# ScalarE's exp planned at its completion rate, accumulator copies on either engine, the tail's range checks in pieces, and the planner's ranks tuned again, in a four-layer attention kernel with a built-in planner

## Chip, cores and metric

One core of a Trainium2 chip. The metric is the device time of one execution in microseconds (us); the kernel before takes **1503.88 us** (median of 3 runs, 1503.73 to 1510.52). A difference under 2% counts as "same", so nearly everything below is about differences that count as the same; some are several times their own noise, some hardly above it, and the text says which.

## The reference, cut

Four residual layers on x (1 x 2048 x 512, bfloat16): two kinds, A and B, in the order A, B, A, B.

```python
x = x + _A_ref(_layernorm(x), A_wqkv, A_wo)   # windowed: 8 keys at distance 2, 32 heads of 16
x = x + _B_ref(_layernorm(x), B_wq, B_wk, B_wv, B_wo)
... # the same two again

def _B_ref(x, wq, wk, wv, wo):                # full attention, 32 heads of 16, one k and v for all
    q = (x @ wq).reshape(B, S, H, Dh).transpose(0, 2, 1, 3)
    k = x @ wk
    v = x @ wv
    scores = jnp.einsum("bhqd,bkd->bhqk", q, k) * (Dh ** -0.5)
    p = _softmax(scores, axis=-1)
    o = jnp.einsum("bhqk,bkd->bhqd", p, v)
    return o.transpose(0, 2, 1, 3).reshape(B, S, H * Dh) @ wo
```

The cost is B: 2 layers x 32 heads x 2048 x 2048 scores and as many exponentials.

## The kernel before

The scores are made in tiles of 128 keys by 512 queries, 4096 of them. A tile is exponentiated in one of two ways: by ScalarE's exp, two tiles an instruction, or by a bit trick: VectorE copies the scores to 16-bit integers, and VectorE or GpSimd adds offsets to them (`do_pass`), so that three shifted sums read as half-precision floats approximate the exponential.

Which tile goes which way, and in which order every engine's instructions are issued, is settled while the program is built. A **planner** in the kernel walks along with a clock for each engine, books each operation at a fixed cost, and always takes the candidate with the lowest start plus bias. The biases ("ranks" from here on) are some fifty tuned numbers. The hardware then runs each engine's list in that order, with semaphores between them; nothing is decided again at run time.

```python
SPAN, ACTIVE = 3413.0, 0.74            # idle matmuls are put in where TensorE is less active than this in such a span
SLACK, PATIENCE = 798.0, 70.6
...
class Stream:
    BIAS = {"act": -50.0, "act2": 1946.7, "vec": 438.1, "pv": 246.6, "pv_in": 177.5, "batch": 17, "few": 19.9,
            "copy": 1.6, "pass": 76.2, "lag": -1045.1, "both": 216.8, "next": 634.6, "late": 31.8, "open": 54.2,
            "close": 4.0}
    ...
    def exp(self, s, _):
        _, key, slot, tiles = self.exps.pop(0)
        n = len(tiles)
        t = 426.7 * n + 52             # the booked cost: 905 ns for two tiles
        S.run("act", s, t)
        done = s + t + LAT["act"]
        S.give(("slot", "exp"), slot, done)
    ...
        # io.exp: nc.scalar.activation(out=pt[:, 0:n, :], in_=st[:, 0:n, :], func=Exp, scale=E_SCALE)
```

A finished accumulator (a PSUM bank of 128 x 512) goes to SBUF; its first part is copied, the others are added:

```python
        def evac(op):
            o = self.o.pop(bank)
            self.chain("dve", nc.vector.tensor_copy(out=X.t[:], in_=o[:]) if fresh else
                       nc.vector.tensor_tensor(out=X.t[:], in0=X.t[:], in1=o[:], op=ALU.add))

        e = X.used(self.op("dve", 599.0, evac, X.prev if fresh else list(X.cur), after=when, frees=[held], prio=-224.4))
```

The approximations hold only in a range of the scores, so the kernel gathers sums and reciprocals (`see`, on GpSimd) and at the very end makes one flag of them, on which an exact fallback branches. Everything behind the last score tile is in `close_tail`:

```python
class Checks:
    def flag_most(self, ok):                       # five flags, one reduction
        ...
        out = [v.tensor_scalar(out=ok[:, at:at + n], in0=x, scalar1=lim, scalar2=None, op0=ALU.is_lt)
               for at, n, x, lim in ((0, 256, self.a[:], self.LOG_A ** 2), (256, 32, self.b[:, 0, :], self.SUM_B),
                                     (288, 32, self.b[:, 1, :], self.REC_B), (320, 512, self.t[:, 0, :], self.SUM_B),
                                     (832, 512, self.t[:, 1, :], self.REC_B))]
        return [*out, v.tensor_reduce(out=self.mb[:, 0:1], in_=ok[:, 0:1344], axis=AX.X, op=ALU.min)]
    ...                                            # flag_last: the last reciprocals' flag and its reduction
    def close_tail(self, a, evac):
        ...                                        # sums by a matmul, Ln, Exp (reciprocal), mult: ons
        self.op("dve", 2300.0, most, [evac, *self.seen, *sees], prio=LATER)
        ...                                        # four output matmuls and their adds
        rec.used(self.op("dve", 1500.0, last, adds))    # flag_last, count (matmul), chk_bad
```

## Time and profile before

| of the kernel before | value | read from |
|---|---|---|
| span of the profiled run | 1500.2 us | head of the page |
| mean granted clock of TensorE | 0.994 | view of the cores |
| exps of two tiles | 1359 | groups |
| tiles by the bit trick | 1378 | groups |
| ScalarE (ACT) idle in all | 1500.2 - 1437.1 = 63.1 us | busy time |

The page's busy times, the groups, the waits and the end of the chain are in the prediction below with their lines.

### The profile page before, as it was taken

Reading aid. Unit: us, or ns where it says so; the run is one execution under the profiler, and the core shown is the slowest. Engines: PE = TensorE matmul, PEld = TensorE weight load, DVE = VectorE, ACT = ScalarE, POOL = GpSimd, SP = SyncE. Lnnn points to the kernel's source line nnn. Section 1 sums busy time; section 2 is a strip of 40 time slices with the busy share of each in tenths; the row PEclk is TensorE's granted clock in tenths of the full one; section 3 lists DMA queues with packets and bytes.
Section 4 is the critical chain, followed back from the end, with each engine's and each line's share of the span. In section 5 each row is a group of like instructions: output and inputs, shape, how many; then the busy total and the mean of one; then the engine's idle time right before and its main releaser. Section 6 shows DMA issues by size and latency. Waiting matters only on the chain.

```text
span 1500.2 us, 42220 instructions
## 1 busy us (share of the span) xinstructions
PE 1430.8 (95%) x17204; PEld 494.9 (33%) x17263; DVE 1339.5 (89%) x2301; ACT 1437.1 (96%) x1754; POOL 896.9 (60%) x741
## 2 busy tenths in 40 slices
PE   8899999999999999999999999999999999999996
PEld 4534343223422233222333224322222222222222
DVE  5787868998799978999789997899999999999997
ACT  6899999999999999999999999999999999999995
POOL 3745546565566656666575664757566656665664
PEclk9999999999999999999999999999999999999999
DMA  4010110011010020100201001001000000000000
GB/s 142 5 29 3 30 16 16 17 31 34 14 23 13 17 38 7 27 13 16 35 13 27 13 15 16 16 9 43 27 12 14 13 23 17 9 18 20 16 9 24
DMA packets 84114, 32.95 MB, mean 22 GB/s; under 512 B 71688, under 2 KB 77448, under 8 KB 83912
## 3 DMA queue, kind: packets, MB, share of 16 engines
q1 hardware_dynamic: 83048, 28.33, 8.8%
q8 instruction: 137, 2.24, 0.6%
q10 hardware_dynamic: 864, 1.84, 0.3%
q14 instruction: 65, 0.53, 0.1%
HBM read 13.53 MB, written 2.61 MB: 11 GB/s over the span
## 4 chain that ended last, share of the span: by engine, by line
ACT 45%; PE 42%; issue 7%; DVE 4%; POOL 1%; DMA 0%; ACTq 0%; POOLq 0%; DVEq 0%
ACT pt L1481 40%; PE o L1507 14%; PE st L1466 14%; PE y L1130 3%; ACT P L1353 2%; PE q L1130 2%; PE k L1130 2%; PE qb L1130 2%; DVE t L1485 2%; PE v L1297 1%; PE dv L1466 1%; ACT logs L1403 1%; ACT rec L1405 1%; PE st L1346 1%; DVE i L1495 1%
## 5 line engine op out<-in xcount | busy, mean ns | idle before, releaser
L1481 ACT ACTIVATE pt<-st 128x1024 bf16<-128x1024 f32 x1359 | 1271.8, 1168 | 16.9 <-PE o L1507 9.1
L1490 POOL TENSOR_TENSOR i<-t,off 128x1024 int32<-128x1024 int32 x345 | 656.2, 1904 | 488.1 <-DVE i L1495 332.7
L1485 DVE TENSOR_SCALAR t<-dv 128x512 int16<-128x512 f32 x1378 | 877.9, 683 | 51.3 <-PE dv L1466 41.5
L1466 PE MATMUL st<-QT,KAB 32*128 32x512 bf16 x1388 | 270.4, 381 | 13.4 <-ACT pt L1481 8.1
L1466 PE MATMUL st<-QT,region 32*128 32x512 bf16 x1330 | 259.1, 379 | 18.4 <-ACT pt L1481 13.9
L1507 PE MATMUL o<-pt,region 128*32 128x512 bf16 x1330 | 270.7, 386 | 0.2
L1507 PE MATMUL o<-i,region 128*32 128x512 f16 x1436 | 265.3, 385 | 1.0 <-DVE i L1495 0.7
L1507 PE MATMUL o<-pt,VEa 128*32 128x512 bf16 x1388 | 261.0, 386 | 0.4 <-DVE x_sb L1429 0.4
L1495 DVE TENSOR_SCALAR i<-t 128x2048 int16<-128x2048 int16 x345 | 238.6, 695 | 3.9 <-PE o L1507 3.1
L1507 PE MATMUL o<-i,VEd 128*32 128x512 f16 x1320 | 240.4, 385 | 0.8 <-POOL i L1490 0.7
L1466 PE MATMUL dv<-QT,region 32*128 32x512 bf16 x718 | 231.5, 382 | 1.0 <-DVE t L1485 1.0
L1466 PE MATMUL dv<-QT,KAB 32*128 32x512 bf16 x660 | 214.6, 383 | 0.0
L1507 PE MATMUL o<-t,region 128*32 128x512 f16 x718 | 181.5, 385 | 0.2 <-DVE t L1485 0.2
L1466 PEld LDWEIGHTS <-region 32*128 32x128 bf16 x2048 | 95.5, 90 | 259.6 <-issue 255.2
L1466 PEld LDWEIGHTS <-KAB 32*128 32x128 bf16 x2048 | 90.7, 90 | 264.4 <-issue 258.0
L1507 PE MATMUL o<-t,VEd 128*32 128x512 f16 x660 | 173.7, 385 | 0.6 <-issue 0.6
L1507 PEld LDWEIGHTS <-region 128*32 128x32 f16 (+1 forms) x3484 | 73.8, 94 | 162.4 <-issue 158.3
L1353 ACT ACTIVATE P<-st 128x576 bf16<-128x576 f32 (+1 forms) x128 | 89.6, 726 | 3.4 <-PE st L1346 3.3
L1507 PEld LDWEIGHTS <-VEd 128*32 128x32 f16 x1980 | 64.4, 94 | 72.6 <-issue 67.7
L1507 PEld LDWEIGHTS <-VEa 128*32 128x32 bf16 x1388 | 58.1, 94 | 79.6 <-issue 77.7
L1360 DVE TENSOR_TENSOR P<-P,bandmask 128x576 int32<-128x576 int32 x64 | 59.0, 926 | 28.3 <-ACT P L1353 26.1
L1414 POOL TENSOR_TENSOR logs<-logs 128x256 f32<-128x256 f32 x64 | 47.5, 742 | 30.2 <-ACT rec L1405 30.2
(173 smaller groups left out, 1180.3 us busy)
## 6 DMA issues: line engine op xcount, KB each, us to landing
lb<-rd SPq DMA_DIRECT2D x31, 256.0 KB
X<-X SPq DMA_DIRECT2D x124, 32.0 KB
k<-oncA SPq DMA_DIRECT2D x48, 64.0 KB
w_sb<-in_A_wqkv_dram ACTq DMA_DIRECT2D x4, 384.0 KB
region<-in_A_x_dram SPq DMA_DIRECT2D x3, 512.0 KB
out_dram<-w_sb SPq DMA_DIRECT2D x3, 512.0 KB
S<-X SPq DMA_DIRECT2D x62, 8.0 KB
rd<-R SPq DMA_DIRECT2D x62, 8.0 KB
```

The lines of the kernel that those rows point to most:

```text
L1130: self.chain("pe", self.nc.tensor.matmul(st["ps"][:], lhsT=lhsT, rhs=rhs, start=first and n == 0, stop=last and n == len(some) - 1))
L1297: self.chain("pe", nc.tensor.matmul(ps[0][64 * a:64 * a + 64, i], lhsT=B.xnT.t[:, kt, kb * 64:(kb + 1) * 64], rhs=wv[:, kt, a, :, :], star ...
L1346: self.chain("pe", nc.tensor.matmul(st[:, j, col:col + w], lhsT=kx[gs], rhs=qt[gs, qbase + q0:qbase + q0 + w], start=True, stop=True, tile ...
L1353: "act", nc.scalar.activation(out=P.t[:, gh, :, c0:UC], in_=self.st.pop(sc)[:, :, c0:UC], func=AF.Exp, scale=DH ** -0.5)), [sc], frees=[sc ...
L1360: self.chain("dve", nc.vector.tensor_tensor(out=x, in0=x, in1=self.w.band[:].unsqueeze(1).to_broadcast([128, 16, NQ // 2]), op=ALU.bitwise ...
L1414: self.chain("pool", nc.gpsimd.tensor_tensor(out=lg.t[:], in0=lg.t[:], in1=lg.t[:], op=ALU.mult))
L1466: self.chain("pe", self.nc.tensor.matmul(out, lhsT=self.KAB[l][32 * g:32 * g + 32, a, kt * 128:(kt + 1) * 128], rhs=self.QT[32 * g:32 * g ...
L1481: self.chain("act", self.nc.scalar.activation(out=self.pt[pt][:, 0:n, :], in_=self.st.pop(key)[:, 0:n, :], func=AF.Exp, scale=E_SCALE))
L1485: self.chain("dve", self.nc.vector.tensor_scalar(out=self.t[buf][:, r, :].bitcast(I16), in0=self.dv[bank][:], scalar1=-U_BIAS, scalar2=U_B ...
L1490: i = self.nc.gpsimd.tensor_tensor(out=self.i[out][:, 0:n, :].bitcast(I32), in0=self.t[buf][:, 0:n, :].bitcast(I32), in1=self.w.off[j][:, ...
L1495: i = self.nc.vector.tensor_scalar(out=self.i[out][:, 0:n, :].bitcast(I16), in0=self.t[buf][:, 0:n, :].bitcast(I16), scalar1=J_OFF[j], sca ...
L1507: self.chain("pe", self.nc.tensor.matmul(self.o[bank][32 * g:32 * g + 32, :], lhsT=lhsT, rhs=rhs, start=first, stop=last, tile_position=(0 ...
```

## The change

Its intent, as far as the diff shows it: ACT's clock in the planner should run as the chip's does; ACT should be able to take an accumulator copy when VectorE is busy; and the checks should not stand between the last sums and the end of the kernel. Whoever made it also tuned the ranks again. The core of the diff:

```diff
-SLACK, PATIENCE = 798.0, 70.6
+SLACK, PATIENCE = 576.3, 2.8
@@ Stream: 14 of the 15 biases, for instance
-    BIAS = {"act": -50.0, "act2": 1946.7, ... "lag": -1045.1, "both": 216.8, "next": 634.6, ...
+    BIAS = {"act": -67.1, "act2": 1808.1, ... "lag": -2657.8, "both": -142.7, "next": 1005.6, ...
-                    idle = max(0.0, s - S.now["act"] - 905.0 * len(self.exps))
+                    idle = max(0.0, s - S.now["act"] - 916.0 * len(self.exps))
-        t = 426.7 * n + 52
+        t = 426.7 * n + 63
@@ close: the first part of an accumulator
-            self.chain("dve", nc.vector.tensor_copy(out=X.t[:], in_=o[:]) if fresh else
-                       nc.vector.tensor_tensor(out=X.t[:], in0=X.t[:], in1=o[:], op=ALU.add))
-        e = X.used(self.op("dve", 599.0, evac, ..., prio=-224.4))
+            if op.eng == "act":
+                self.chain("act", nc.scalar.copy(out=X.t[:], in_=o[:]))
+            else:
+                ...  # as before
+        e = X.used(self.op({"act": act_ns(512), "dve": 599.0} if fresh else {"dve": 599.0}, 0, evac, ..., prio=-40.3))
@@ close_tail: flag_most and flag_last become operations of their own
+            small = self.op("dve", 560.0, lambda op: chain(flag(a), flag(b0), flag(b1)), [*chk.seen, ...], prio=LATER)
+            wide = [self.op("dve", 410.0, ... flag(t[n]) ..., [seen[n], ...], prio=LATER, port=("dve",)) for n, lim in ...]
+            half = self.op("dve", 800.0, ... all_of(ok[:, 0:672]) ..., [small, *wide], prio=LATER)
+            self.most = self.op("dve", 800.0, ... all_of(ok[:, 672:1345]) ..., [half], prio=LATER)
...
+        own = self.op("dve", 1050.0, ... flag and reduction of the last sums ..., [evac, self.most])
+        mine = rec.used(self.op("dve", 1050.0, ... of the last reciprocals ..., [re, own, *ons], prio=FIRST))
+        n = self.op("pe", 60.0, ... count ..., [mine], ...)
+        self.op("dve", 140.0, ... chk_bad ..., [n], prio=SOON)
-        self.op("dve", 2300.0, most, [evac, *self.seen, *sees], prio=LATER)
-        rec.used(self.op("dve", 1500.0, last, adds))
@@ some thirty ranks of single operations, for instance the scores of layer A
-                         solid=True, mode="row", prio=-265.3 + self.PRIO)
+                         solid=True, mode="row", prio=-272.1 + self.PRIO)
```

## The prediction

> **What bounds the kernel now.** I began with the page: busy time by engine, then the costliest groups.
>
> ```profile
> PE 1430.8 (95%) x17204; PEld 494.9 (33%) x17263; DVE 1339.5 (89%) x2301; ACT 1437.1 (96%) x1754; POOL 896.9 (60%) x741
> ...
> ACT 45%; PE 42%; issue 7%; DVE 4%; POOL 1%; DMA 0%; ACTq 0%; POOLq 0%; DVEq 0%
> ...
> L1481 ACT ACTIVATE pt<-st 128x1024 bf16<-128x1024 f32 x1359 | 1271.8, 1168 | 16.9 <-PE o L1507 9.1
> ...
> L1485 DVE TENSOR_SCALAR t<-dv 128x512 int16<-128x512 f32 x1378 | 877.9, 683 | 51.3 <-PE dv L1466 41.5
> ```
>
> The work is 4096 score tiles of 128x512. A tile goes either through ScalarE's exp (two tiles an instruction, 1359 of them, 2718 tiles) or through the bit trick on VectorE and GpSimd (1378 tiles). A planner written into the kernel chooses tile by tile, with a fixed cost for each instruction, and issues what it planned in a fixed order. ACT and PE both look full, so I asked who waits for whom. The view of waits says that score matmuls wait for exps 102 times, and exps for matmuls far less:
>
> ```profile
> PE st L1466 <- ACT pt L1481: 22.0, 102, 0.5
> ...
> ACT pt L1481 <- PE o L1507: 9.1, 14, 1.3
> ```
>
> Then the busy time by stretch (columns: PE, PEld, DVE, ACT, POOL) and ACT's timeline:
>
> ```profile
> 50.00:200.00 150.00, 141.85 (x2204) 58.48 (x2204) 117.55 (x212) 136.01 (x199) 83.05 (x95) 0.97 0.09 16
> 200.00:1000.00 800.00, 773.13 (x9719) 267.83 (x9751) 713.51 (x1209) 784.82 (x966) 485.45 (x390) 1.00 0.10 20
> 1000.00:1450.00 450.00, 434.42 (x4194) 130.73 (x4198) 438.88 (x734) 447.88 (x489) 280.67 (x178) 1.00 0.07 18
> ...
> 1484.60:1500.20 15.60, 5.46 (x24) 2.55 (x25) 7.61 (x16) 1.38 (x4) 1.26 (x1) 0.79 0.11 38
> ```
>
> ```profile
> 1059.21 150.66 ACT L1481 ACTIVATE pt<-st 128x1024 bf16<-128x1024 f32 x164 [0.54 <-PE o L1507]
> 1211.17 239.85 ACT L1481 ACTIVATE pt<-st 128x1024 bf16<-128x1024 f32 x261 [1.30 <-PE o L1507]
> ```
>
> From 1000 us on ACT runs nothing but exps and is idle 2.1 us of 450: **ACT is the bound**, with DVE close behind (438.9 of 450). Earlier ACT has gaps: 15.2 us in 200 to 1000, 14.0 in 50 to 200. One exp costs 239.85 / 261 = 919 ns in such a run, 917 ns without the last one's latency. The mean duration of 1168 ns is no cost, since each starts before the one ahead ends. The planner before books 2 x 426.7 + 52 = 905 ns, 12 ns too little: 1359 x 12 = 16 us over the kernel by which its clock for ACT falls behind the chip's.
>
> The end is a stage of its own, bound by a chain. Its view from 1484 us on (start, length, what):
>
> ```profile
> 1487.26 0.76 DVE w_sb L1652 x2
> 1488.02 1.05 DVE i L864 x5
> 1489.07 0.02 issue
> 1489.10 1.56 DVE chk_mb L868
> 1490.65 2.38 DVE w_sb L1623 x4
> 1493.04 0.35 DVE i L872
> 1493.39 0.02 issue
> 1493.41 0.70 DVE chk_mb L873
> 1494.11 0.04 issue
> 1494.15 0.18 PE chk_cnt L877
> 1494.33 0.02 issue
> 1494.35 0.15 DVE chk_bad L878
> ```
>
> The flag is known at 1494.50; the load of it, the branch and the closing take the 5.7 us to 1500.2. The output's last packets land at 1494.4 by the trace's DMA records, so this chain ends the kernel and not the stores.
>
> **What the Trainium skill says.** "ScalarE: Activation LUTs", section What ACT_TABLE_LOAD costs, gives an ACTIVATE with immediate scale and bias 186 ns + 0.833 ns a column, less about 93 ns back to back: an estimate from it of 946 ns for 1024 columns. The trace has 917, so the measurement decides; the new 916 matches it. "Perfetto Trace Analysis", section Optimizing Scalar/DVE Operations, gives ScalarE about 51 ns of access overhead on PSUM: 853 + 51 = 904, the old plan's number. The trace shows that too, but as the most common spacing of starts; ends come 916 to 917 apart. The same page, section Identifying the Most-Contended Engine, warns that matmul busy time is a poor measure and points to weight loads: PE is 95% by the one and 33% by the other, and it waits for ACT, so I don't take PE as the bound. "SBUF — State Buffer", section SBUF: two separate sides, says that the shared port pair of VectorE and GpSimd is an exclusive lock; that matters as the change adds passes on both. Here POOL stands idle before its passes 488 us in all, mostly on DVE passes, with 40% of its time free.
>
> **The change part by part.** The order of instructions of both programs (no time in it) gives the counts.
>
> 1. Exps: 1359 of two tiles become 1347 and one of a single tile. Saved on ACT: 12 x 0.917 less 0.49 (an estimate: one 512-column instruction at the spacing of the 512-column casts) = 10.5 us.
> 2. First accumulator parts: 6 of 64 copies from PSUM go to ACT. A 512-column copy there ends 0.477 us after the one ahead when they queue: +2.9 us on ACT, -6 x 0.598 = -3.6 us on DVE.
> 3. Small evacuations change engines: ACT gets 4 QT and 6 q more, 6 k and 4 v fewer (0), 2 transposes' copies fewer (-1.0), one scaled copy more (+0.6), one norm fewer (-0.7), one tiny one fewer (-0.1): -1.2 us.
>    ACT in sum: -10.5 + 2.9 - 1.2 = **-8.8 us**.
> 4. VectorE gets 23 tiles more (0.598 apart in a queue: +13.8 us), 6 passes of 2048 more at 0.60 with a small remainder (+3.5), less the copies (-3.6), and about +1.8 of moved small ones: +15.5 us. It idles 160 us, but only 11 of that after 1000 us. The counts say that 18 of the 23 tiles belong to the first attention layer (the K operand KAB), before about 846 us, where DVE is at 89%. GpSimd: 6 passes more at 1.85, about +10 us of its 600 idle.
> 5. PE: each moved tile has two matmuls more, 46 in 17204. Nothing.
> 6. The tail. Before, five flags and a reduction (1.05 + 1.58 us) stand between the last normalization and the four sums, and another flag, reduction and count (1.25 us) behind them. After, the order has the first group in the stream ahead of the last tiles, the flags of the last sums while ACT works on the reciprocal, and only one flag and one reduction (0.35 + 0.70) ahead of the four sums. The sums can't start before their matmul, whose first ended at about 1489.3, against 1488.02 + 1.05 = 1489.07 for the flags. So 1489.4 + 2.4 for the sums + 0.2 for the last comparison = 1492.0, against 1494.5: **-2.5 us**. The last store would then land near 1493.2, before the closing asks for it.
> 7. Priorities: no operation, only order. With ACT's clock right, the plan's idea of when a PSUM slot frees agrees with the chip, and some of the 33 us of ACT gaps between 50 and 1484 us (150 - 136.0, 800 - 784.8, 2.1, and 2.2 in the last stretch) can close. I book 1.5 us for it, a guess.
>
> Sum: 1503.9 - 8.8 - 2.5 - 1.5 = **1491 us**.
>
> **The rivals.** (a) **VectorE takes over as the bound.** If the added tiles fall where DVE is full (49 of 50 us from 1000 us on), ACT gets gaps behind PE instead. Against it: only 5 of the added tiles belong to the second layer, 3.7 us of DVE by 0.75 us each, inside its 11 us of slack. Then the saving of step 1 is mostly lost: about 1499. (b) **The retuned order opens new gaps early.** Between 50 and 200 us the chain goes through PE, GpSimd and ACT in turn; another ranking can add gaps as easily as remove them: 1497 to 1503. For it: dozens of priorities move at once, and the old plan was already tuned. (c) **The plan's drift was the real loss**, PE's order being wrong by up to 16 us at the end, so that the true clock closes most of the 33 us: 1470 to 1480. Against it: ACT is without gaps just where the drift is largest, after 1000 us; a wrong clock cost it nothing there. (d) **The tail gives nothing**, because 2.4 us of checks now stand on DVE ahead of the last partial pass, and delay the last matmuls: 2.5 us lost, about 1493.5.
>
> **Range and chances.** The tally of ACT is firm (an instruction count by a measured spacing); how far the gaps change isn't. Halving the 33 us gives 1476, adding 8 us gives 1500. Weighing those as tails, I take 1483 to 1499 for 8 in 10. Faster by over 2% means below 1473.8, which needs nearly all gaps closed besides: 0.03. Slower by over 2% needs a broken plan: 0.01.
>
> **What would show it.** Step 1: exps 1348 and still 917 to 919 ns apart in long runs, ACT busy about 1428 us, its idle from 50 us to the tail near 32. Step 4: DVE busy near 1354, waits of PE for exps no longer than 22 us. Step 6: the comparison that makes the flag starts some 7.3 us after the last accumulator matmul ends (before: 9.8), directly behind the fourth sum. Wrong it would be if ACT shows more idle between 50 and 1484 us than now (rival b or a, told apart by whether DVE is full there), or much less (c).

## The result, and the profile after

The changed kernel takes **1499.91 us** (median of 5 runs, 1499.12 to 1502.51), the kernel before in the same rounds 1503.88 (5 runs, 1502.89 to 1510.52). The ratio is **0.9966** [0.9943, 0.9989]. A ratio here is the mean time of one kernel's runs over the mean of the other's in the same rounds, so it is not quite the ratio of the medians. So the change is a gain, of 4 us and not of 13: within 2% was right, and the time lies 0.9 us above the range.

The page of the changed kernel: busy time by engine, shares of the chain that ended last, and the two groups that the prediction counted (busy us, mean ns of one, then idle time ahead of them).

```profile
PE 1449.7 (97%) x17270; PEld 484.4 (32%) x17329; DVE 1360.2 (91%) x2332; ACT 1429.5 (95%) x1746; POOL 904.3 (60%) x744
...
PE 61%; ACT 27%; DVE 6%; issue 4%; POOL 2%; ACTq 0%; DVEq 0%; POOLq 0%
...
L1477 ACT ACTIVATE pt<-st 128x1024 bf16<-128x1024 f32 x1348 | 1262.9, 1142 | 16.8 <-PE o L1503 5.7
...
L1481 DVE TENSOR_SCALAR t<-dv 128x512 int16<-128x512 f32 x1401 | 889.0, 682 | 41.9 <-PE dv L1462 36.3
```

ACT is busy 1429.5 us, VectorE 1360.2, and 23 tiles have moved: as predicted. The view of waits and ACT's timeline:

```profile
PE st L1462 <- ACT pt L1477: 7.6, 37, 0.5
```

```profile
1062.42 148.19 ACT L1477 ACTIVATE pt<-st 128x1024 bf16<-128x1024 f32 x161 [0.27 <-PE dv L1462]
```

Scores wait for exps 7.6 us where they waited 22.0, and the exps keep their pace: 148.19 / 161 = 920 ns. All that agrees with the prediction. Yet the span fell only from 1500.2 to 1498.2 in the two profiled runs: ACT's busy time by 7.6 us, and its idle time **rose** by 5.6 (63.1 to 68.7). Where, the busy time of ACT by stretch tells. Columns: stretch, its length, ACT busy (instructions), granted clock, share of DMA, GB/s. Before:

```profile
0.00:50.00 50.00, 34.63 (x64) 1.00 0.34 108
...
100.00:200.00 100.00, 93.15 (x127) 0.98 0.10 18
200.00:300.00 100.00, 98.20 (x128) 1.00 0.11 19
300.00:1400.00 1100.00, 1084.50 (x1272) 1.00 0.09 20
```

After:

```profile
0.00:50.00 50.00, 30.77 (x55) 0.91 0.35 108
...
100.00:200.00 100.00, 91.50 (x126) 0.98 0.10 18
200.00:300.00 100.00, 94.46 (x125) 1.00 0.11 18
300.00:1400.00 1100.00, 1087.40 (x1275) 1.00 0.09 20
```

Busy less by 3.9 + 1.7 + 3.7 us, and 0.1 in the stretch left out: by 300 us the changed kernel has 9.4 us more of gaps, 40.6 against 31.2. From 300 to 1400 us it has 2.9 less. The saving was to come out of the whole stream, but ACT's remaining work at 300 us is the same in both (1169 us, within 2): 18 of the 23 moved tiles belong to the first half of the tiles, 12 of them to the first eighth. So half of the work was taken off just where ACT was already waiting for others, and the new gaps there, 9.4 us in this profile, are larger than all that was saved (7.6). The 500th tile is finished at 303.0 us (before: 297.9), the 3950th of 4096 at 1435.8 (before: 1438.0), the last at 1483.4 (before: 1483.1): the middle gains, and the last 146 tiles lose the lead again.

The tail, in the chain of work that ended last (start, length, what):

```profile
1479.84 2.37 DVE xnT L864 x2
1482.20 0.77 DVE xnT L867
...
1483.86 0.21 DVE i L1491
...
1484.86 0.38 PE o L1503
...
1489.91 2.53 DVE w_sb L1622 x4
1492.44 0.06 DVE chk_bad L874
```

The comparison that makes the flag starts directly behind the fourth sum (1489.91 + 2.53 = 1492.44). The last accumulator matmul ended at 1485.24, so 7.26 us passed up to the end of that comparison, where the kernel before took 9.92: step 6 in itself was right within 0.2 us. But the lines above show what the prediction had as rival (d): the flags (`xnT L864`) and reductions (`L867`) are on the chain ahead of `DVE i L1491`, which is VectorE's **last pass** of the bit trick, for which the last matmuls wait. And the flags are not short. GpSimd's timeline, then VectorE's, both of the changed kernel:

```profile
1468.03 1.94 POOL L1486 TENSOR_TENSOR i<-t,off 128x1024 int32<-128x1024 int32 x1
...
1480.01 1.91 POOL L1486 TENSOR_TENSOR i<-t,off 128x1024 int32<-128x1024 int32 x1 [1.10 <-PE o L1503]
```

```profile
1468.14 1.95 DVE L864 TENSOR_SCALAR xnT<-chk_b 128x32 bf16<-128x32 f32 x2
...
1479.75 2.45 DVE L864 TENSOR_SCALAR xnT<-oncA 128x512 bf16<-128x512 f32 x2
```

And the flags one by one, the shortest, median and longest duration in ns, in the view of that source line; before, then after:

```profile
L864 DVE TENSOR_SCALAR i<-chk_b x2: 174/174/175, 1488.1 to 1488.2; 128x32 bf16<-128x32 f32 x2
L864 DVE TENSOR_SCALAR i<-oncA x2: 421/421/421, 1488.3 to 1488.6; 128x512 bf16<-128x512 f32 x2
```

```profile
L864 DVE TENSOR_SCALAR xnT<-chk_b x2: 168/1017/1866, 1468.1 to 1469.9; 128x32 bf16<-128x32 f32 x2
L864 DVE TENSOR_SCALAR xnT<-oncA x2: 420/1269/2118, 1479.8 to 1480.1; 128x512 bf16<-128x512 f32 x2
```

A flag of 32 columns, 174 ns before, takes up to 1866 ns (the pair 1.95 us) and one of 512 columns 2118 instead of 421. In each pair one flag is as fast as before, and the one that starts while GpSimd's pass runs ends just behind it: the first small one at 1470.01 us (the pass: 1468.03 + 1.94 = 1469.97), the second wide one at 1482.20 (the pass: 1480.01 + 1.91 = 1481.92). Moved into the stream, a flag meets GpSimd's passes and stands behind them with everything that VectorE has to do next.

**A source of spread.** The record of TensorE's granted clock shows pieces at half speed, 3.4 us long or a multiple of it, at other places in each run. The same eight idle matmuls at 10.6 us took 1.90 us in the profiled run before and 3.46 in the one after. All engines in the stretch 10.6 to 14.0 us (columns PE, PEld, DVE, ACT, POOL; then clock, DMA, GB/s), before, then after:

```profile
10.60:14.00 3.40, 2.91 (x21) 1.44 (x19) 2.66 (x7) 2.37 (x4) 1.21 (x5) 1.00 0.62 166
```

```profile
10.60:14.00 3.40, 3.40 (x11) 1.25 (x9) 2.66 (x7) 1.30 (x2) 1.21 (x5) 0.53 0.58 154
```

It is not of one kernel: the 23 runs of the kernel before with a clock fall in a row by their mean clock, from 1506.8 us at 0.990 to 1499.8 at 0.997. One slope for all 98 such runs of the 14 kernels, with a level for each kernel, gives **1.00 us per 0.001 of mean clock** and leaves 0.9 us of scatter. (That the slope is common to all is assumed; each kernel's few runs alone give 0.6 to 1.4.) With it I give each result also "at equal clock": the difference from the kernel before, clock taken out, good to some 0.9 us, and to some 1.2 us between two other versions. The changed kernel itself is then 4.8 us faster than the kernel before.

### The profile page after: what moved, and what is told of

Its sections match the earlier page's. It is cut to its first block, busy times and chain, and to the rows that moved or that the text cites. A ratio compares the mean times of both kernels' runs of the same rounds, so it can differ in the third digit from the quotient of the medians.

```text
span 1498.2 us, 42436 instructions
## 1 busy us (share of the span) xinstructions
PE 1449.7 (97%) x17270; PEld 484.4 (32%) x17329; DVE 1360.2 (91%) x2332; ACT 1429.5 (95%) x1746; POOL 904.3 (60%) x744
## 4 chain that ended last, share of the span: by engine, by line
PE 61%; ACT 27%; DVE 6%; issue 4%; POOL 2%; ACTq 0%; DVEq 0%; POOLq 0%
PE o L1503 24%; ACT pt L1477 23%; PE st L1462 20%; PE dv L1462 3%; PE y L1126 3%; DVE t L1481 3%; ACT P L1349 2%; PE q L1126 2%; PE k L1126 2%; PE qb L1126 2%; PE v L1293 1%; ACT logs L1399 1%; DVE i L1491 1%; PE st L1342 1%; PE oa L1369 1%
## 5 line engine op out<-in xcount | busy, mean ns | idle before, releaser
L1486 POOL TENSOR_TENSOR i<-t,off 128x1024 int32<-128x1024 int32 x351 | 666.1, 1899 | 477.9 <-DVE i L1491 306.7
L1481 DVE TENSOR_SCALAR t<-dv 128x512 int16<-128x512 f32 x1401 | 889.0, 682 | 41.9 <-PE dv L1462 36.3
L1462 PE MATMUL st<-QT,KAB 32*128 32x512 bf16 x1370 | 266.6, 382 | 8.1 <-ACT pt L1477 5.1
L1503 PE MATMUL o<-pt,VEa 128*32 128x512 bf16 x1370 | 255.6, 387 | 1.0 <-DVE t L1481 0.9
L1503 PE MATMUL o<-i,VEd 128*32 128x512 f16 x1356 | 246.3, 385 | 0.7 <-POOL i L1486 0.7
L1491 DVE TENSOR_SCALAR i<-t 128x2048 int16<-128x2048 int16 x351 | 241.4, 690 | 1.8 <-PE o L1503 1.1
L1462 PE MATMUL dv<-QT,region 32*128 32x512 bf16 x723 | 240.1, 381 | 2.0 <-DVE t L1481 1.9
L1462 PE MATMUL dv<-QT,KAB 32*128 32x512 bf16 x678 | 221.1, 382 | 0.2 <-DVE t L1481 0.2
L1462 PEld LDWEIGHTS <-KAB 32*128 32x128 bf16 x2048 | 82.5, 91 | 254.0 <-issue 251.0
L1462 PEld LDWEIGHTS <-region 32*128 32x128 bf16 x2048 | 86.1, 90 | 242.5 <-issue 240.2
```

What stands on the lines that cost most here:

```text
L1462: self.chain("pe", self.nc.tensor.matmul(out, lhsT=self.KAB[l][32 * g:32 * g + 32, a, kt * 128:(kt + 1) * 128], rhs=self.QT[32 * g:32 * g ...
L1481: self.chain("dve", self.nc.vector.tensor_scalar(out=self.t[buf][:, r, :].bitcast(I16), in0=self.dv[bank][:], scalar1=-U_BIAS, scalar2=U_B ...
L1486: i = self.nc.gpsimd.tensor_tensor(out=self.i[out][:, 0:n, :].bitcast(I32), in0=self.t[buf][:, 0:n, :].bitcast(I32), in1=self.w.off[j][:, ...
L1491: i = self.nc.vector.tensor_scalar(out=self.i[out][:, 0:n, :].bitcast(I16), in0=self.t[buf][:, 0:n, :].bitcast(I16), scalar1=J_OFF[j], sca ...
L1503: self.chain("pe", self.nc.tensor.matmul(self.o[bank][32 * g:32 * g + 32, :], lhsT=lhsT, rhs=rhs, start=first, stop=last, tile_position=(0 ...
```

## The experiments

Two explanations stood at the start. **The order:** retuned ranks and a true clock make another order, whose opening has more gaps, and the checks delay the last pass. **The clock:** the changed kernel loses time to half-clock pieces in its opening, and the order is as good as predicted. In the expectations Theory 1 is the checks, Theory 2 the clock, Theory 3 what made the opening's gaps (the ranks in rate_only, the rate in after_oldrate), and Theory 4, which came later, that a plan is a lottery. Twelve kernels, five rounds each: six runs with the profiled one, only four of before_53. The last four (after_62 to retuned) ran on another chip than the first eight, where the kernel before is 0.5 us faster at equal clock (the chip of the change's own five runs is not on record). All gave correct results. Results in short:

| kernel | median us | before, same rounds | ratio [95%] | at equal clock, us |
|---|---|---|---|---|
| the change | 1499.91 | 1503.88 | 0.9966 [0.9943, 0.9989] | -4.8 |
| after_oldtail | 1497.98 | 1504.3 | 0.9975 [0.9951, 0.9999] | -5.7 |
| after_latecheck | 1496.74 | 1504.3 | 0.9958 [0.9934, 0.9982] | -7.5 |
| after_awake | 1497.36 | 1504.3 | 0.9962 [0.9942, 0.9983] | -4.5 |
| rate_only | 1508.44 | 1504.3 | 1.0034 [1.0014, 1.0054] | +4.6 |
| before_newtail | 1501.7 | 1501.69 | 1.0001 [0.9963, 1.004] | +1.0 |
| before_awake | 1504.62 | 1501.69 | 1.0013 [0.9986, 1.0041] | +2.3 |
| after_oldrate | 1508.3 | 1501.69 | 1.0034 [1.0017, 1.0051] | +3.7 |
| after_dvecopy | 1505.98 | 1501.69 | 1.0016 [0.9993, 1.0039] | +1.5 |
| after_62 | 1512.08 | 1502.69 | 1.006 [1.0037, 1.0083] | +6.5 |
| after_64 | 1508.53 | 1502.69 | 1.0037 [1.0023, 1.0051] | +5.1 |
| before_53 | 1519.74 | 1502.69 | 1.012 [1.0102, 1.0138] | +13.1 |
| retuned | 1501.81 | 1502.69 | 0.9983 [0.9966, 1.0001] | -6.0 |

### after_oldtail: the change without its tail

```diff
 # the changed kernel, with Checks and close_tail of the kernel before
-            small = ...; wide = ...; half = ...; self.most = ...
+        self.op("dve", 2300.0, most, [evac, *self.seen, *sees], prio=LATER)
...
+        rec.used(self.op("dve", 1500.0, last, adds))
```

> The kernel after with the end of the kernel before (all range checks behind the last accumulator copy); every order before 1466 us is the same. Theory 1 (checks put into the stream hold VectorE up behind GpSimd and cost what the shorter end gains): the last accumulator matmul ends 2 to 4 us earlier than the 1485.2 of after, its wait of VectorE for GpSimd at 1468 and 1480 is gone, the chain from there to the flag is back at 9.9 us, and the time is 1499 to 1500, as after. Rival (the new end is worth its predicted 2.5 us): 1502.4.

Measured: 1497.98 us, ratio 0.9975; at equal clock 5.7 us faster than the kernel before, 0.9 faster than the change. So the new tail, in which the prediction saw 2.5 us of gain, brings none, as Theory 1 had it, and the rest of the change is worth 5.7 us where the prediction had 8.8 + 1.5 = 10.3. In the profiled runs the last accumulator copy ends at 1481.6 us with the old tail and at 1485.9 with the new; the flag then comes 8.7 and 6.6 us later. The new tail is shorter, and begins later. (Two single profiled runs at different clocks; the difference of 0.9 us rests on all the runs, and is within its error of some 1.2.)

### after_latecheck: the same checks behind the last pass

```diff
-            small = self.op(... [*chk.seen, *self.xnT.cur], prio=LATER)
-            wide = ...; half = ...; self.most = ...           # placed by rank among the last tiles
+        flags = self.op("dve", 1100.0, lambda op: chain(... the five flags ...),
+                        [*chk.seen, *self.seen, *self.xnT.cur], after=evac.after - 500.0)
+        most = self.op("dve", 1460.0, lambda op: chain(chk.all_of(chk.mb[:, 0:1], ok[:, 0:1344])), [flags])
+        own = self.op("dve", 350.0, lambda op: chain(chk.flag(ok[:, 1344:1856], X.t[:], chk.SUM_B)), [evac, most])
+        # last: one scalar_tensor_tensor (is_lt, then min) joins both last flags, one reduction behind it
```

> The kernel after with its early checks moved to just behind VectorE's last pass, and the last reduction joined with that of the sums. Theory 1: the last accumulator matmul ends 2 to 4 us earlier, the chain behind it takes 7.5 to 8 us, so 1496.5 to 1498. Rival (checks in the stream cost nothing): the same as after or up to 1 us slower, 1500 to 1501.

Measured: 1496.74 us, ratio 0.9958, at equal clock 7.5 us faster than the kernel before and 2.7 faster than the change: the best, its fastest run at 1493.07. VectorE's timeline of this kernel:

```profile
1476.10 1.95 DVE L864 TENSOR_SCALAR xnT<-chk_b 128x32 bf16<-128x32 f32 x2
```

The two small flags are blocked just as long, 1.95 us. But now no pass stands behind them: they lie in the time in which VectorE only waits for the last matmuls. The last accumulator copy ended at 1480.5 us and the flag came 6.9 us later. That shows rival (d) from the other side: the prediction's 2.5 us were there to be had, with the checks behind the last pass and not ahead of it.

The profiles of seven versions say the same without any correction for the clock. From the end of the 3950th tile to the end of the last accumulator matmul it takes 46.1 to 46.6 us in the four that have no check in the stream (before, before_awake, after_oldtail, after_latecheck) and 49.0 to 49.4 in the three that have them there (the change, after_awake, before_newtail): **some 3 us, no less than the 2.0 to 2.6 us that the shorter end gains**. Behind that matmul, after_latecheck needs 7.6 us to the flag, the three 7.3, the old end 9.3 to 9.9.

### after_awake and before_awake: more idle matmuls against the clock

```diff
-SPAN, ACTIVE = 3413.0, 0.74
+SPAN, ACTIVE = 3413.0, 0.95      # 360 idle matmuls instead of 276 in the changed kernel; same order otherwise
```

> The kernel after with the planner's idle matmuls allowed up to 0.95 instead of 0.74 of its window: the same order of all real work, 360 idle matmuls instead of 276, only in planned gaps of TensorE. Theory 2 (the halved TensorE clock, 20 us in after against 10 in before, makes the new gaps of ScalarE in the first 300 us): the drops at 44, 167 and 1471 us shrink or go, ScalarE's idle time up to 300 us falls from 40.6 to 35 or less, time 1495 to 1497. Rival (the new order makes the gaps): 40 us of idle stay, 1499 to 1501.

> The kernel before with idle matmuls up to 0.95 of the window (350 instead of 256), the order of all real work as before. Theory 2 (the halved clock costs what it covers): the drops at 53 and 115 us go, with the 2.7 and 0.8 us of ScalarE gaps found there; 2 to 4 us faster, ratio 0.9975 to 0.9985; ScalarE's idle up to 300 us falls from 31.2 to 28. So it gains about what after gained from the same edit, and the difference of the two plans stays. Rival (only the kernel after suffers from the clock): the same as before within 1 us.

Measured: the changed kernel becomes 1497.36 us (ratio 0.9962), and its mean clock 0.9937 where it was 0.9914. At equal clock it is -4.5 us, against -4.8: the whole difference is the clock's. For the kernel before, the same edit gives 1.0013 [0.9986, 1.0041], 2.3 us worse at equal clock; 2 to 4 us faster was expected, so Theory 2 missed there. The profiled run of after_awake had the full clock in its first 100 us, so it shows the changed order without half-clock pieces there:

```profile
0.00:50.00 50.00, 33.36 (x61) 1.00 0.34 108
50.00:100.00 50.00, 44.55 (x78) 1.00 0.06 13
100.00:200.00 100.00, 90.55 (x124) 0.97 0.12 20
200.00:300.00 100.00, 94.39 (x125) 1.00 0.09 17
```

ACT is busy 262.85 of these 300 us, so idle 37.1, against 31.2 before and 40.6 in the change's own profile. The expectation named 35 or less or 40: neither came. About 3.5 of the 9.4 us of new gaps may thus be luck of the clock in one run. The other versions with one of these two openings agree: ACT is idle by 300 us for 31.0, 31.2 and 34.2 us with the old order (before_newtail, before, before_awake) and for 37.1, 38.1, 38.4 and 40.6 with the new one (after_awake, after_latecheck, after_oldtail, the change). Three of them have the same 10.2 us of half clock by then: 31.0 and 31.2 with the old order, 38.1 with the new. So **some 6 to 7 us are the order's**. The gap from 200 to 300 us (94.39 busy; before 98.20) does not move at all. The clock explains the spread between runs and not why the change gives less than predicted. Whether more idle matmuls make half-clock pieces rarer stays open: one kernel got a higher mean clock with them, the other no better a time.

### rate_only and after_oldrate: the booked rate alone, and everything but the rate

```diff
 # rate_only: the kernel before with        # after_oldrate: the changed kernel with
-... - 905.0 * len(self.exps)               -... - 916.0 * len(self.exps)
+... - 916.0 * len(self.exps)               +... - 905.0 * len(self.exps)
-        t = 426.7 * n + 52                 -        t = 426.7 * n + 63
+        t = 426.7 * n + 63                 +        t = 426.7 * n + 52
```

> The kernel before with the exp planned 11 ns longer, and nothing else of the change; it has 1349 exps of two tiles and 2 of one (before 1359, after 1347 and 1), so about 8 us less of ScalarE's work. Theory 3 (the retuned ranks, not the rate, made the gaps of the first 300 us): idle by 300 us stays near the 31 us of before, time 1496 to 1498. Rival (whatever is moved from ScalarE returns as gaps): 1501 to 1504, with idle time 8 us larger.

> The kernel after with the exp booked at 905 ns again; its ranks, its end and its copies stay; 1359 exps of two tiles and 1 of one. Theory 3 (the rate makes the opening gaps: booked short, ScalarE comes late to everything it waits for and finds it ready): idle of ScalarE by 300 us 31 to 34, end of the stream as in before, time 1501 to 1504. Rival (the new ranks make them): idle by 300 us 38 or more, and with the exps not moved, 1506 or more.

Measured: rate_only 1508.44 us, ratio 1.0034, **4.6 us slower** than the kernel before at equal clock; after_oldrate 1508.3, ratio 1.0034, 3.7 slower. Together they are 4.8 us faster. Neither time expected for rate_only came; for after_oldrate the rival's did. (Of rate_only's 4.6 us, 1.6 lie outside the span of its instructions: its device time is 3.3 us above its span, in all others 1.7. I have no reason for it.) The true rate does what the prediction counted, in numbers: rate_only issues 1349 exps of two tiles where the kernel before has 1359, and ACT is busy 1431.3 us against 1437.1. But ACT is idle 71.6 us, 38.8 of them by 300 us. (after_oldrate: 38.1 by 300 us. So the opening's gaps come with the new rate and the old ranks, and with the old rate and the new ranks; neither alone is what makes them.) Its largest single wait from 200 to 300 us, in ACT's timeline:

```profile
264.37 0.21 ACT L1103 CAST VEa<-vp 128x64 bf16<-128x64 f32 x1 [5.67 <-PE vp L1450]
```

ACT runs its list in order. This cast of the values stands ahead of the next exps in the list, and waits for matmuls on TensorE. What they read comes by four transposing transfers, the last of which landed at 263.4 us; the matmuls ahead of them in TensorE's list waited for a GpSimd pass until 263.4 as well, so either may have held them. Before, the longest such wait in that stretch is 0.7 us. So one small instruction whose place in the list came out too early stops ACT for the time of six exps. That is the mechanism in one example; the gaps of after_oldrate and of the change are spread over many shorter waits (in the change, 2.2 us and 1.9 us are the largest sums in that stretch), and which of them bounds the opening I did not settle.

### before_newtail: the tail alone

```diff
 # the kernel before, with Checks and close_tail of the changed kernel; nothing else
```

> The kernel before with the new end alone: checks in pieces in the stream, one flag and one reduction ahead of the four sums; every other order and cost is that of before. Theory 1: the chain from the last accumulator matmul to the flag shrinks from 9.9 to about 7.3 us, but the checks in the stream are held up behind GpSimd as in after and give back 1 to 3 us of it: 1 us faster to 1 us slower than before. Rival (the new end is worth its 2.5 us in full): 2.5 us faster, a ratio of 0.998.

Measured: ratio 1.0001 [0.9963, 1.004], at equal clock 1.0 us slower. With after_oldtail (0.9) that is the same finding from two sides: as written, the new tail gains nothing and may cost up to 1 us. Each figure alone is near its error; the 2.5 us of gain that step 6 booked are excluded by both.

### after_dvecopy: first accumulator parts by VectorE only

```diff
-        e = X.used(self.op({"act": act_ns(512), "dve": 599.0} if fresh else {"dve": 599.0}, 0, evac, ...
+        e = X.used(self.op({"dve": 599.0}, 0, evac, ...
```

> The kernel after with all first accumulator parts copied by VectorE; 1356 exps of two tiles and 1383 tiles by VectorE, so the plan gives ScalarE back what the copies took. Theory: the choice is worth little, 1499 to 1502. Rival (it is what let the plan move the exps, and so the part that matters): as slow as before or slower, 1504 to 1508.

Measured: 1505.98 us, ratio 1.0016, 1.5 us slower than the kernel before at equal clock, so 6.3 slower than the change. Six copies of some 0.5 us cannot be worth that by their own time. The planner without this freedom makes another plan: 1357 exps and 1383 tiles on VectorE instead of 1348 and 1401. So the time is the rival's, but the result measures that plan, not the copies.

### after_62, after_64 and before_53: one nanosecond

```diff
-        t = 426.7 * n + 63     # the changed kernel, 916 ns          # before: + 52
+        t = 426.7 * n + 62     # after_62; after_64: + 64            # before_53: + 53
```

(The same 1 ns in the line with 916 and 905.)

> The kernel after with the exp booked one nanosecond shorter, 915 instead of 916 ns; the planner's own end moves by +8.6 us (1488.5 instead of 1479.9), 1349 exps of two tiles. Theory 4 (the plan is a lottery that the ranks were drawn for: at the true rate a plan takes its own end plus what it took in after): 7 to 10 us slower than after at equal clock, 3 to 5 us slower than before, a ratio of 1.002 to 1.004. Rival (the rate works through the share of the engines, smoothly): within 1 us of after, a ratio of 0.996 to 0.998.

> The kernel after with the exp booked one nanosecond longer, 917 ns; the planner's own end moves by +8.8 us to 1488.7, 1350 exps. Theory 4: 7 to 10 us slower than after at equal clock. Rival: within 1 us of after.

> The kernel before with the exp booked one nanosecond longer, 906 ns; the planner's own end moves by +15.9 us to 1490.6. Theory 4: 12 to 16 us slower than before, a ratio of 1.008 to 1.011, the largest step of all, from the smallest edit. Rival (smooth): within 1 us of before.

Measured, at equal clock: the changed kernel goes from -4.8 us to **+6.5** with 1 ns less and to **+5.1** with 1 ns more; the kernel before loses **13.1** with 1 ns more (ratio 1.012 [1.0102, 1.0138], four runs). One nanosecond is 0.1% of an exp and cannot matter by itself. Theory 4 holds for after_64 and before_53; after_62 lost 11.3 us, more than the 7 to 10 expected. Both kernels sit on a narrow point: another rate gives another plan. That their ranks were tuned for one exact plan, and that every other plan is of untuned quality, would explain it, and is not shown. But a step of 5 us or less says nothing about the rate, if 1 ns makes one of 10 to 13: rate_only (+4.6) and after_oldrate (+3.7) lose no more than any other move off these points, and it is the **pair**, rate and ranks, that was changed.

Does the true rate do anything, then? The planner's own end, the time at which its book closes, set against the chip at one clock of 0.994:

| kernel | booked exp, ns | planner's end, us | chip, us | chip - planner |
|---|---|---|---|---|
| before | 905 | 1474.7 | 1502.4 | 27.7 |
| after_oldrate | 905 | 1479.7 | 1506.1 | 26.4 |
| before_53 | 906 | 1490.6 | 1515.4 | 24.8 |
| rate_only | 916 | 1489.6 | 1507.0 | 17.4 |
| the change | 916 | 1479.9 | 1497.6 | 17.7 |
| after_dvecopy | 916 | 1485.5 | 1503.8 | 18.3 |
| after_62 | 915 | 1488.5 | 1508.9 | 20.4 |
| after_64 | 917 | 1488.7 | 1507.5 | 18.8 |
| after_oldtail | 916 | 1481.6 | 1496.7 | 15.1 |
| after_latecheck | 916 | 1479.7 | 1494.9 | 15.2 |
| retuned | 916 | 1476.4 | 1496.4 | 20.0 |

At the old rate the book closes 25 to 28 us too early, at the true one 15 to 20: a shift of about 9 us, of the 15 us that 1359 exps of 11 ns add up to. And within one rate the planner's end agrees with the chip on which plan is better to within some 2.5 us either way. By this table the kernel before and the change differ by 5.2 us in the plan for the worse, and the chip pays it back with 10 us less of surprises. The planner's end is itself jagged, which is the one-nanosecond result again without a chip: the ranks of the kernel before give 1478.0, 1474.7 and 1490.6 us for +51, +52 and +53.

### retuned: can the book be trusted below 3 us?

```diff
 # after_latecheck with ten ranks from a random search on the planner's own end, for instance
-            ... "few": 26.2, ... "lag": -2657.8, ... "next": 1005.6, ... "close": 8.5}
+            ... "few": 29.9, ... "lag": -2788.0, ... "next": 1024.6, ... "close": 5.7}
```

> The kernel after_latecheck with ten of the planner's numbers found by a random search on the planner's own end at the true rate (1476.4 instead of 1479.7); exp still booked at 916 ns. Theory 4: 3.3 us faster than after_latecheck at equal clock, so some 11 us faster than before, a ratio near 0.9928, the fastest of all. Rival (the planner's end says nothing below 5 us): anywhere within 5 us of after_latecheck.

Measured: 1501.81 us, ratio 0.9983 [0.9966, 1.0001]. At equal clock it is 6.0 us faster than the kernel before, but 1.5 **slower** than after_latecheck (error some 1.2, and on another chip, so hardly slower), where the planner's end had promised 3.3 faster. A miss, and within the rival's 5 us: the search found a plan that is good in the book, and the last 3 us of the book are not the chip's. For such sizes only the chip can choose.

## Why the prediction was right or wrong

Right, by its own steps: the counts and costs. ACT busy 1429.5 us ("about 1428"), VectorE 1360.2 ("near 1354"), 1348 exps at an unchanged pace, waits for exps under 22 us, and 7.2 us from the last accumulator matmul to the start of the flag's comparison ("some 7.3"). Within 2% was right. "PE: Nothing" held in instructions (66 more in the trace, 20 of them idle matmuls), but TensorE's busy time rose by 18.9 us. (The 904 ns that the prediction works out as 853 + 51 is, like its 946, an estimate from a page's figure.)

Wrong was the sum: -12.8 us, where the runs show -4.8 at equal clock. One of its own signs of being wrong came too: ACT's idle time from 50 to 1484.6 us is 37.8 us, where it was 33.5 and "near 32" was expected. The 8.0 us that are missing lie in two places.

- **"Sum: 1503.9 - 8.8 - 2.5 - 1.5": the stream, 4.6 us.** The prediction took the 8.8 us of saved ACT work off the end one for one, and 1.5 more for gaps that would close. Measured on after_oldtail, this part is worth 5.7, not 10.3. The work was indeed saved (7.6 us in the trace). But half of it (12 of the 23 tiles) was saved in the first 300 us, while the prediction's reason for calling ACT the bound was the stretch from 1000 us on, where exps and gaps stayed as they were (489 exps, idle 1.4 us for 2.1). In the opening ACT has gaps of its own, and with the new order they grew (by some 6 to 7 us over seven profiles, 9.4 in the change's own). That is rival (b), whose 1497 to 1503 us held the result, though the steadiest of the new gaps lies from 200 to 300 us, later than it looked. The prediction even had the fact in hand: step 4 counts 18 of 23 moved tiles in the first attention layer, and used it only to clear VectorE.
- **"6. The tail ... -2.5 us": 3.4 us.** The length of the tail was right, its start was not. The checks that left the tail stand on VectorE ahead of its last pass, twice held up by 1.7 us behind a GpSimd pass; the last accumulator matmul ends some 3 us later for it. Rival (d) named it, with the right sign; net it cost nothing to 1 us. after_latecheck shows it by taking the cause away: 2.7 us back, with the same checks.
- **Step 7, "With ACT's clock right, the plan's idea ... agrees with the chip"**, was a guess of 1.5 us, and its premise holds in part: planner and chip do come nearer, by 9 us. But a plan that is nearer to the truth is not a better plan: with the rate alone changed the time was 4.6 us worse, and any other plan might have been.

Rival (a), VectorE as the bound, did not come: VectorE has 444.1 of 450 us from 1000 us on, but ACT is idle 1.4 us there. Rival (c), that drift was the real loss, did not come either: at the true clock ACT's idle time from 300 to 1400 us fell by 2.9 us, not by most of 33.

What stays open: which wait bounds the first 300 us; why the chain that ended last is now 61% PE, and whether TensorE, busy 445.4 of 450 us from 1000 us on (before: 434.4), took part of the gain (not tested); and why both kernels are so much better than their neighbours at 1 ns. The planner's end has the same steps (8.6, 8.8 and 15.9 us for after_62, after_64 and before_53; on the chip 11.3, 9.9 and 13.1), so most of each step is in the plan already, but that gives no reason. That the ranks were chosen by times on a chip would explain it, and is only argued. The best version measured is after_latecheck, 0.9958 of the kernel before.

## What to carry to other kernels

Saved work counts only in the stretch where its engine is the bound: look up in which stretch the saved instructions lie, and what the engine waits for there, before subtracting them from the end. A constant in a planner cannot be judged apart from the numbers tuned around it: move it by its least step first, and if the time jumps by 10 us there, as it did twice here, a test of "this part alone" measures the tuning and not the part. Work moved off a tail onto a shared engine goes behind the last thing that others wait for, not ahead of it.

## What the Trainium skill lacked or had wrong

- "SBUF — State Buffer", section SBUF: two separate sides, gives the exclusive lock between VectorE and GpSimd, and the page has sizes for a transfer that is held up and a factor of 6.8 for VectorE, but no time for a short VectorE instruction that loses. Here a 32-column comparison went from 174 to 1866 ns, and one of 512 columns from 421 to 2118, ending 0.04 and 0.28 us behind the GpSimd pass of 1.9 us that they met. A small instruction costs up to the other engine's whole pass.
- "TensorE: Matmul & The Clock Gate", Part 1, describes the half clock and its window of about 3.4 us, which the trace's pieces of 3.4, 6.8 and 10.2 us agree with. It says that the slow start varies from run to run, and what such windows cost where waits recur in a kernel; it does not say that in one busy program they fall at other places, and in other numbers, in each run: here mean clocks of 0.990 to 0.997 for one kernel, at 1.00 us per 0.001. A comparison of less than 0.5% has to take that out.
- "ScalarE: Activation LUTs", section What ACT_TABLE_LOAD costs, leads to an estimate of 946 ns for back-to-back ACTIVATEs of 1024 columns; both traces have 917 to 920 in runs without gaps.
- No page warns that a tuned static order is a narrow point: 1 ns in a booked duration of 916 or 905 moved the time by 10 to 13 us.
